# One row of exponentials per batch on ScalarE in a fused attention, gated and soft mixture kernel

## The chip, the core and the metric

One core of a Trainium2 chip runs the kernel. Its engines are TensorE (PE in the profile; PEld is its weight loads), VectorE (DVE), ScalarE (ACT), GpSimd (POOL) and SyncE (SP), which issues the DMAs here. The metric is the device time of one execution in microseconds; lower is better. Spans and rows of a profile come from one execution that the hardware profiler recorded.

## The reference

Three stages follow one another. Shapes: x is 8 batches, 8 heads, 512 tokens, 64 wide; state has 32 rows per batch and head.

```
scores  = x @ state^T / 8                 # per batch and head, 512 x 32
a       = softmax(scores, over the 32)    ; xread = a @ state
a2      = softmax(scores^T, over the 512) ; sread = a2 @ x
X       = [xread ; sread], 4352 tokens of 512
xn      = X / rms(X) * g
Y       = (silu(xn @ w_gate) * (xn @ w_val)) @ w_out     # 512 -> 1536 -> 512
logits  = Y @ phi                          # 32 slots, 4 for each of 8 experts
d       = softmax(logits, over all tokens) ; slots = d^T @ Y
out_e   = relu(slots_e @ w1_e) @ w2_e
result  = softmax(logits, over the 32 slots) @ out
```

Both softmaxes over many rows subtract a maximum first; the one over all tokens is kept as a running maximum and sum, batch by batch.

## The kernel before, in words

The work goes by batch g (a group of 512 tokens, four tiles of 128). The kernel never forms Y's input rows in full: it multiplies the attention weights A of a batch with a product of state and weights. For each batch and each of three column parts c of w_gate and w_val, `sw(b, c, gv)` makes that product in two PSUM banks; ScalarE copies each bank into the high part of a tile wp, and VectorE subtracts to get the low part, after which the banks are empty. `main_mm` (six matmuls) then makes one 128 x 512 tile of gate or val; `main_silu` (sg, on ScalarE) and `main_h` (h, on VectorE) empty it. `h_T` ("turn") transposes h by TensorE, and ScalarE or VectorE copies the result into hT. `lg_mm` gives the logits of a batch, `post1`, `post2`, `post_exp`, `post3` the running softmax (lgs is a copy of the logits, L their slots, nm the negated maximum, E the exponentials, al the factor for what came before), and `slot_h` adds to the slot sums acc on VectorE. `c_exp` and `c_norm` make the softmax over the slots.

Attention of a later batch is woven in: `att_a3` makes the scores in two banks and takes their maximum cm and a copy sT; `att_a4` makes a transposed copy a and subtracts block maxima; `att_exp` exponentiates sT and a; `att_norm` normalizes; `att_b1` turns sT into e2T; `att_b2`, `att_b3` give the state read; `att_gram`, `att_q`, `att_v`, `att_ss`, `rinv` give the rms. `wconv` converts one piece of w_out, on ScalarE, VectorE and GpSimd.

For batches 2 to 7 `steady(g)` lays a stage out by hand. A stage has 12 units (c, t); a unit is one gate and one val `main_mm`. After every second unit comes a burst, `bursts[0]` to `bursts[5]`, and `plan` puts further steps at a unit. Within these stages TensorE takes its instructions in the order of the program text (`manual_schedule`). On the other engines a scheduler fixes the order at compile time: an instruction that is ready earlier may go first, and among ready ones the one traced first. `tc.keep_in_program_order(ins)` ("pin") holds an instruction behind the one traced just before it on its engine; it doesn't hold later ones back. There are four `misc` banks (sw, turns, and all small products) and three `mm` banks (main_mm) in PSUM, and 19 buffers of 8 KB per partition, k8, for wp, h, hT and the loads. The exponential and silu use different tables of ScalarE, and a load of a table stands in the trace as ACT_TABLE_LOAD under the line of the activation that wants it.

Of the kernel before, what the change touches and what calls it, by code (L numbers as in the profile page):

```python
# [12 lines left out]
AF = mybir.ActivationFunctionType  # L13
ALU = mybir.AluOpType
AX = mybir.AxisListType
# [5 lines left out]
def kernel(  # L21
# [16 lines left out]
    nc = tc.nc  # L38
    B, P, H, NT, D = x_n.shape
# [6 lines left out]
    NC = DFF // 512  # L46
    NF = DFF // P
    ROWS = S + NS
    scale = 1.0 / float(D) ** 0.5
# [16 lines left out]
    def k4(name, shape, dt=F32):  # L66
        return att.tile([P] + shape, dt, tag="k4", bufs=5, name=name)

    def asmall(name, shape, bufs=1, dt=F32):
        return att.tile(shape, dt, tag=name, bufs=bufs, name=name)  # L70
# [4 lines left out]
    def small(name, shape, bufs=1, dt=F32):  # L75
        return sm.tile(shape, dt, tag=name, bufs=bufs, name=name)
# [4 lines left out]
    def misc():  # L81
        return psp.tile([P, 512], F32, tag="misc", bufs=4, name="misc")

    def mm(o, lhsT, rhs, start=True, stop=True):
        nc.tensor.matmul(out=o, lhsT=lhsT, rhs=rhs, start=start, stop=stop)  # L85
# [24 lines left out]
    def transpose(o, i):  # L110
        nc.tensor.transpose(o, i, ident)  # L111


    XN, T = {}, {}
# [126 lines left out]
    def att_a3(b):  # L241
        sT = k4("sT", [2, 512])
        cm = asmall("cm", [P, 2], bufs=2)
        ncm = asmall("ncm", [P, 2], bufs=2)
        pss = [misc(), misc()]
        for r in range(2):
            for hp in range(4):
                mm(
                    pss[r][32 * hp : 32 * hp + 32, :],
                    T[b, "stT"][64 * r : 64 * r + 64, 32 * hp : 32 * hp + 32],  # L250
                    T[b, "xT"][64 * r : 64 * r + 64, hp, :],
                )
            if b == 0:
                nc.scalar.copy(sT[:, r, :], pss[r])
            nc.vector.reduce_max(cm[:, r : r + 1], pss[r], axis=AX.X)
            if b > 0:
                nc.scalar.copy(sT[:, r, :], pss[r])
        nc.vector.tensor_scalar(
            out=ncm, in0=cm, scalar1=-scale, scalar2=None, op0=ALU.mult
        )  # L260
        T[b, "sT"], T[b, "ncm"] = sT, ncm

    def att_a4(b):
        sT = T[b, "sT"]
        if b > 0:
            a = k4("a", [2, 16, 32])
            rm = asmall("rm", [P, 32], bufs=2)
            nc.vector.transpose(
                a.rearrange("p r t n -> p (r t n)"), sT.rearrange("p r s -> p (r s)")
            )  # L270
            a3 = a.rearrange("p r t n -> p (r t) n")
            nc.vector.reduce_max(rm, a3, axis=AX.X)
            nc.gpsimd.tensor_tensor(
                out=a3, in0=a3, in1=rm.unsqueeze(2).to_broadcast([P, 32, 32]), op=ALU.subtract
            )
            T[b, "a"] = a
            return
        a = k4("a", [NT, 2, 4, 32])
        rm = asmall("rm", [P, NT, 2, 4], bufs=2)
        for j in range(2):  # L280
            ps = misc()
            for t2 in range(2):
                t = 2 * j + t2
                for r in range(2):
                    o = (2 * t2 + r) * P
                    transpose(ps[:, o : o + P], sT[:, r, t * P : (t + 1) * P])
            v = ps.rearrange("p (t r k n) -> p t r k n", t=2, r=2, k=4)
            rmj = rm[:, 2 * j : 2 * j + 2]
            nc.vector.reduce_max(rmj, v, axis=AX.X)
            nc.vector.tensor_tensor(  # L290
                out=a[:, 2 * j : 2 * j + 2].rearrange("p t r k n -> p (t r k) n"),
                in0=ps.rearrange("p (a n) -> p a n", n=32),
                in1=rmj.rearrange("p t r k -> p (t r k)").unsqueeze(2).to_broadcast([P, 16, 32]),
                op=ALU.subtract,
            )
        T[b, "a"] = a.rearrange("p t r k n -> p t r (k n)")
# [314 lines left out]
    def gsize(g):  # L611
        return 2 if g == sread_group else NT
# [29 lines left out]
        )  # L642
        Q[g, "L"], Q[g, "nm"], Q[g, "dm"] = L, nm, dm

    def post_exp(g):
        np_ = gsize(g) * 32
        L, nm, dm = Q[g, "L"], Q[g, "nm"], Q[g, "dm"]
        E = small("E", [P, P])
        es = small("es", [P, 1], bufs=2)
        nc.scalar.activation(  # L650
            out=E[:np_], in_=L[:np_], func=AF.Exp, bias=nm[:np_], accum_out=es[:np_]
        )
        if g > 0:
            al = small("al", [P, 1], bufs=2)
            nc.scalar.activation(out=al[:np_], in_=dm[:np_], func=AF.Exp)
            nc.vector.scalar_tensor_tensor(  # L656
                out=sacc[:np_], in0=sacc[:np_], scalar=al[:np_], in1=es[:np_],
                op0=ALU.mult, op1=ALU.add,
            )
            Q[g, "al"] = al  # L660
        else:
            nc.vector.tensor_copy(sacc, es)
        Q[g, "E"] = E
# [242 lines left out]
    def steady(g):  # L906

        nb, nn = g + 1, g + 2
        last = g == B - 1

        def turn(c, t, dve=False):
            return (h_T, g, c, t, dve)

        bursts = [[] for _ in range(6)]
        b = bursts[0]
        if g > 2:
            b += [(lg_mm, g - 1, 2, 3), (post1, g - 1)]
        b += [turn(0, 0, True), (sw, g, 1, 0), (post2, g - 1)]
        if not last:
            b += [(att_gram, nb)]  # L920
        b += [(post_exp, g - 1), (c_exp, g - 2, True)]
        b = bursts[1]
        b += [(sw, g, 1, 1)]
        if 2 < g < B - 1:
            b += [(att_b2, g)]
        b += [turn(0, 1), (post3, g - 1), turn(0, 2)]
        if not last:
            b += [(att_b1, nb)]
        b = bursts[2]
        b += [turn(0, 3), turn(1, 0)] + [(slot_h, g - 1, i) for i in range(NC)]  # L930
        if 2 < g < B - 1:
            b += [(att_b3, g)]
        if g == B - 2:
            b += [(att_b2, nb)]
        b += [(lg_mm, g, 0, 3), (sw, g, 2, 0)]
        b = bursts[3]
        b += [(sw, g, 2, 1)]
        if not last:
            b += [(att_q, nb, 0), (att_q, nb, 1)]
        b += [turn(1, 1), turn(1, 2)]  # L940
        if g == B - 2:
            b += [(att_b3, nb)]
        b = bursts[4]
        if nn < B:
            b += [(att_a3, nn)]
        b += [turn(1, 3)]
        if not last:
            b += [(att_v, nb), (att_ss, nb), (rinv, nb), (sw, nb, 0, 0)]
        else:
            b += [turn(2, 0)]  # L950
        if g == B - 2:
            b += [(sread_sum,)]
        b = bursts[5]
        if not last:
            b += [(sw, nb, 0, 1), turn(2, 0), (lg_mm, g, 1, 3), turn(2, 1), turn(2, 2), turn(2, 3, True)]
            if g == B - 2:
                b += [(sread_prep2,)]
            ended.add(g)
        else:
            b += [turn(2, 1), (lg_mm, g, 1, 3), turn(2, 2)]  # L960

        at = lambda u, slot, f, *a: plan.setdefault((base + u, slot), []).append((f, a))
        at(2, 1, c_norm, g - 2)
        if not last:
            at(1 if g == B - 2 else 7, 1, load_xn, nb)
            at(1, 1, att_exp, nb, True)
            at(2, 1, att_norm, nb)
            at(4, 1, att_b4, nb)
            at(6, 1, att_g, nb)
            at(1, 1, wload, 1)  # L970
            at(4, 1, wconv, 1)
        if nn < B:
            at(8, 1, load_xt, nn)
            at(9, 1, att_z, nn)
            at(11, 1, att_a4, nn)
        if g == B - 2:
            at(8, 1, sread_prep)
        if last:
            at(0, 2, prefetch, 2)
            at(8, 1, prefetch, 2)  # L980
            at(11, 1, w_split, 0, 0)
            at(12, 2, w_split, 1, 0)

        return bursts

    for s, units in enumerate(stages):
        def at(u, slot, f, *a):
            plan.setdefault((base + u, slot), []).append((f, a))
# [65 lines left out]
        elif s == 1:  # L1054
            g = s
# [9 lines left out]
            nb = g + 1  # L1065
# [14 lines left out]
            nb = g + 2  # L1080
# [4 lines left out]
        else:  # L1085
            if s == 2:
                pe_order.enter_context(tc.manual_schedule(engines={mybir.EngineType.PE}))
            bursts = steady(s)
# [56 lines left out]
    for u, (c, gv) in enumerate(halves):  # L1145
# [56 lines left out]
        out=dsel, in0=mg, scalar1=mrun, scalar2=0.0, op0=ALU.subtract, op1=ALU.max  # L1202
# [45 lines left out]
    for e in range(NE):  # L1248
        es = slice(4 * e, 4 * e + 4)
        nc.vector.tensor_tensor(  # L1250
            out=sinE[e][:, :, es],
            in0=ps[:, :P].rearrange("p (k s) -> p k s", k=4)[:, :, es],
# [164 lines left out]
    def out0_end(t, ps, copy):  # L1417
# [15 lines left out]
        out=so[64:], in0=ps[64:], in1=so_h[64:].bitcast(F32), op=ALU.subtract  # L1433
# [58 lines left out]
```

## Time and profile before

| what | us |
|---|---|
| median of three runs | 664.88 (663.0 to 666.22) |
| the profiled execution, its own time | 665.96 |
| its span in the profile | 664.1 |

The granted clock of TensorE is 0.97 of full speed over the span. The stages of batches 2 to 7 lie between about 190 and 545 us of the span; the stage of batch 4 begins near 309.5, that of batch 7 near 486.5. A row of the timeline gives start, duration (of all that is merged in it), engine, line, operation, what is written from what, the count, and in brackets how long the engine had been idle and what ended that.

### The profile page before, as it was taken

The page shows a single profiled execution, that of the slowest core. Times are in us where ns is not written, and L with a number is a line of the kernel's source. Part 1 is how long each engine was busy: PE and PEld are TensorE (multiplying, and loading weights), DVE is VectorE, ACT ScalarE, POOL GpSimd, SP SyncE. Part 2 cuts the span into 40 slices and gives each one's busy share as a digit, 9 for nine tenths or more (in the row PEclk, how much of TensorE's full clock was granted, in tenths as well). Part 3 has the DMA queues.
Part 4 walks back from the last instruction along what each step waited for, and adds up shares of the span by engine and source line. Part 5 has one row for each costly group of instructions (what it writes and reads, how often), then busy time and mean ns, then how long its engine had stood idle before and what let it go on. Part 6 is the DMA issues. An engine that isn't in the chain of part 4 may idle for free.

```text
span 664.1 us, 11195 instructions
## 1 busy us (share of the span) xinstructions
PE 613.4 (92%) x4432; PEld 386.4 (58%) x4432; DVE 437.3 (66%) x874; ACT 349.5 (53%) x558; POOL 157.3 (24%) x178
## 2 busy tenths in 40 slices
PE   6679988899998999999999999999999999999990
PEld 4336555456566556666656656666765777653350
DVE  6979999576587776766868585685765365252161
ACT  5467773475268447534843763484346476311170
POOL 2645455342032311401141040113000000003420
PEclk9697999799999999999999999999999999999996
DMA  8950065131020410031040104300270327999757
GB/s 354 416 207 1 1 254 191 63 127 68 1 81 16 163 51 14 21 143 64 1 164 12 53 1 159 128 1 34 102 279 3 126 84 274 318 332 402 301 207 331
DMA packets 32715, 92.14 MB, mean 139 GB/s; under 512 B 1816, under 2 KB 3224, under 8 KB 29848
## 3 DMA queue, kind: packets, MB, share of 16 engines
q1 hardware_dynamic: 32376, 91.36, 37.2%
q8 instruction: 35, 0.57, 0.4%
q14 instruction: 16, 0.13, 0.1%
q10 hardware_dynamic: 288, 0.07, 0.0%
HBM read 79.37 MB, written 12.06 MB: 138 GB/s over the span
## 4 chain that ended last, share of the span: by engine, by line
PE 68%; DVE 11%; ACT 7%; issue 2%; POOL 0%; DVEq 0%; ACTq 0%
PE mm L85 38%; PE misc L85 15%; PE misc L111 9%; PE lg L85 4%; PE so L85 2%; DVE wp L538 2%; DVE h L574 1%; DVE w L204 1%; ACT L566 1%; ACT sg L566 1%; ACT wp L537 1%; ACT L650 1%; DVE wo L204 1%; DVE sacc L656 1%; DVE w L212 1%
## 5 line engine op out<-in xcount | busy, mean ns | idle before, releaser
L85 PE MATMUL mm<-wp,A 128*128 128x512 f32 x1152 | 286.3, 401 | 3.8 <-DVE h L574 2.4
L85 PEld LDWEIGHTS mm<-wp,A 128*128 128x128 f32 x1152 | 213.3, 190 | 75.4 <-issue 23.4
L574 DVE SCALAR_TENSOR_TENSOR h<-mm,rinv,sg 128x512 f32<-128x512 f32 x102 | 76.0, 747 | 87.3 <-PE mm L85 81.8
L566 ACT ACTIVATE sg<-mm,rinv 128x512 f32<-128x512 f32 x102 | 70.5, 692 | 103.0 <-PE mm L85 90.7
L537 ACT CAST wp<-misc 128x512 fp32r<-128x512 f32 x96 | 51.5, 590 | 65.3 <-PE misc L85 65.3
L538 DVE TENSOR_TENSOR wp<-misc,wp 128x512 fp32r<-128x512 f32 x96 | 62.2, 684 | 24.8 <-ACT wp L537 24.7
L85 PE MATMUL misc<-w,stTg 64*32 64x512 f32 x768 | 67.1, 626 | 12.0 <-POOL w L216 6.6
L585 ACT COPY hT<-misc 128x512 f32<-128x512 f32 x87 | 48.9, 591 | 41.3 <-PE misc L111 35.5
L111 PEld LDWEIGHTS misc<-ident,h 128*128 128x128 f32 x408 | 45.7, 142 | 32.3 <-DVE h L574 10.6
L111 PE MATMUL misc<-ident,h 128*128 128x128 f32 x408 | 59.1, 282 | 4.0 <-ACT hT L585 2.1
L216 POOL TENSOR_TENSOR w<-w,raw 128x512 int32<-128x512 int32 x20 | 28.3, 1426 | 29.2 <-DVE w L212 7.1
L85 PEld LDWEIGHTS misc<-w,stTg 64*32 64x32 f32 x768 | 10.9, 106 | 37.1 <-issue 15.4
L85 PE MATMUL mm<-wh,xsg 128*128 128x512 f32 x96 | 31.8, 400 | 0.0
L511 POOL TENSOR_TENSOR rinv<-ri,rs_magic 128x4 int32<-128x4 int32 (+1 forms) x9 | 1.8, 197 | 122.1 <-DVE ri L507 122.0
L216 POOL TENSOR_TENSOR wo<-wo,raw 128x512 int32<-128x512 int32 x18 | 24.7, 1385 | 22.7 <-DVE wo L212 7.0
L468 POOL TENSOR_TENSOR A<-aT,A 128x1024 fp32r<-128x1024 f32 x7 | 16.9, 2411 | 46.1 <-ACT A L467 46.1
L85 PE MATMUL lg<-hT,wphi 128*32 128x512 f32 (+1 forms) x216 | 27.5, 579 | 0.0
L85 PE MATMUL misc<-h,ET 128*32 128x512 f32 x204 | 26.4, 596 | 0.0
L1238 POOL MEMSET sinE<- 128x512 f32 x2 | 1.0, 524 | 106.2 <-PE mm L85 96.1
L566 ACT ACT_TABLE_LOAD x18 | 23.1, 1283 | 0.3
L191 ACT ACTIVATE raw<-raw 128x1024 int32<-128x1024 uint32 x19 | 22.1, 1161 | 0.0
L85 PEld LDWEIGHTS mm<-wh,xsg 128*128 128x128 f32 x96 | 17.9, 188 | 6.7 <-issue 3.1
(221 smaller groups left out, 845.2 us busy)
## 6 DMA issues: line engine op xcount, KB each, us to landing
ew<-in_w_dram SPq DMA_DIRECT2D x27, 1024.0 KB, 6.7
xT<-in_x_t_dram SPq DMA_DIRECT2D x8, 1024.0 KB, 7.6
xn<-in_x_n_dram SPq DMA_DIRECT2D x8, 1024.0 KB, 6.4
raw<-in_w_val_dram SPq DMA_DIRECT2D x6, 1024.0 KB, 15.9
raw<-in_w_out_dram SPq DMA_DIRECT2D x6, 1024.0 KB, 5.1
out_dram<-ob SPq DMA_DIRECT2D x6, 1024.0 KB, 10.4
ew_w<-in_w_dram SPq DMA_DIRECT2D x5, 1024.0 KB, 9.3
raw<-in_w_gate_dram SPq DMA_DIRECT2D x4, 1024.0 KB, 13.8
```

The costliest lines, as they stand in the source:

```text
L85: nc.tensor.matmul(out=o, lhsT=lhsT, rhs=rhs, start=start, stop=stop)
L111: nc.tensor.transpose(o, i, ident)
L191: ins = nc.scalar.activation(out=rnd, in_=lo.bitcast(U32), func=AF.Copy, scale=2.0 ** -29)
L204: nc.vector.tensor_scalar(out=dst[:, h], in0=dst[:, h], scalar1=EXP_LO, scalar2=EXP_HI, op0=ALU.max, op1=ALU.min,)
L212: nc.vector.scalar_tensor_tensor(out=a[:, h], in0=hi[:, h], scalar=-0x40000000, in1=a[:, h], op0=ALU.bitwise_and, op1=ALU.bitwise_or,)
L216: nc.gpsimd.tensor_tensor(out=a[:, h], in0=a[:, h], in1=rnd[:, h], op=ALU.add)
L468: nc.gpsimd.tensor_tensor(out=A[:, :, 1, :], in0=aT, in1=A[:, :, 0, :].bitcast(F32), op=ALU.subtract)
L537: nc.scalar.copy(t[:, r, 0, :], ps)
L538: nc.vector.tensor_tensor(out=t[:, r, 1, :], in0=ps, in1=t[:, r, 0, :].bitcast(F32), op=ALU.subtract)
L566: nc.scalar.activation(out=sg, in_=ps, func=AF.Silu, scale=RINV[g][:, t : t + 1])
L574: nc.vector.scalar_tensor_tensor(out=HH[g, c][:, t, :], in0=ps, scalar=RINV[g][:, t : t + 1], in1=sg, op0=ALU.mult, op1=ALU.mult,)
L585: (nc.vector.tensor_copy if on_dve else nc.scalar.copy)(HT[g, c][:, :, t * P : (t + 1) * P], ps.rearrange("p (q n) -> p q n", q=4))
```

## The change

In `steady`, `sw(g, 1, 0)` becomes the first step of the first burst and `sw(g, 1, 1)` moves from the second burst into the first. `post_exp` is pinned; attention's exponentials for the next batch (`att_exp`) move from the plan of unit 1 to a place right behind it, ahead of `c_exp`. The second burst keeps `att_b2`, one turn, whose copy goes from ScalarE to VectorE, and `post3`, and gets `sw(g, 2, 0)` from the third. The third burst interleaves turns and slot products and takes `att_b1`. In batch 6's stage the state read of the last batch, its preparation and its sums move one burst later. For batches 4 to 7 (`b > 3`) `att_a3` only copies the scores; the maximum, over both halves in one instruction, is taken from the copy in `att_a4`. For batches 1 to 3 the maximum is taken as before.

```diff
--- before.py
+++ after.py
@@ -252,13 +252,15 @@
                 )
             if b == 0:
                 nc.scalar.copy(sT[:, r, :], pss[r])
-            nc.vector.reduce_max(cm[:, r : r + 1], pss[r], axis=AX.X)
+            if b <= 3:
+                nc.vector.reduce_max(cm[:, r : r + 1], pss[r], axis=AX.X)
             if b > 0:
                 nc.scalar.copy(sT[:, r, :], pss[r])
-        nc.vector.tensor_scalar(
-            out=ncm, in0=cm, scalar1=-scale, scalar2=None, op0=ALU.mult
-        )
-        T[b, "sT"], T[b, "ncm"] = sT, ncm
+        if b <= 3:
+            nc.vector.tensor_scalar(
+                out=ncm, in0=cm, scalar1=-scale, scalar2=None, op0=ALU.mult
+            )
+        T[b, "sT"], T[b, "ncm"], T[b, "cm"] = sT, ncm, cm
 
     def att_a4(b):
         sT = T[b, "sT"]
@@ -274,6 +276,12 @@
                 out=a3, in0=a3, in1=rm.unsqueeze(2).to_broadcast([P, 32, 32]), op=ALU.subtract
             )
             T[b, "a"] = a
+            if b > 3:
+                cm = T[b, "cm"]
+                nc.vector.reduce_max(cm, sT, axis=AX.X)
+                nc.vector.tensor_scalar(
+                    out=T[b, "ncm"], in0=cm, scalar1=-scale, scalar2=None, op0=ALU.mult
+                )
             return
         a = k4("a", [NT, 2, 4, 32])
         rm = asmall("rm", [P, NT, 2, 4], bufs=2)
@@ -642,17 +650,21 @@
         )
         Q[g, "L"], Q[g, "nm"], Q[g, "dm"] = L, nm, dm
 
-    def post_exp(g):
+    def post_exp(g, pin=False):
         np_ = gsize(g) * 32
         L, nm, dm = Q[g, "L"], Q[g, "nm"], Q[g, "dm"]
         E = small("E", [P, P])
         es = small("es", [P, 1], bufs=2)
-        nc.scalar.activation(
+        ins = nc.scalar.activation(
             out=E[:np_], in_=L[:np_], func=AF.Exp, bias=nm[:np_], accum_out=es[:np_]
         )
+        if pin:
+            tc.keep_in_program_order(ins)
         if g > 0:
             al = small("al", [P, 1], bufs=2)
-            nc.scalar.activation(out=al[:np_], in_=dm[:np_], func=AF.Exp)
+            ins = nc.scalar.activation(out=al[:np_], in_=dm[:np_], func=AF.Exp)
+            if pin:
+                tc.keep_in_program_order(ins)
             nc.vector.scalar_tensor_tensor(
                 out=sacc[:np_], in0=sacc[:np_], scalar=al[:np_], in1=es[:np_],
                 op0=ALU.mult, op1=ALU.add,
@@ -913,34 +925,37 @@
 
         bursts = [[] for _ in range(6)]
         b = bursts[0]
+        b += [(sw, g, 1, 0)]
         if g > 2:
             b += [(lg_mm, g - 1, 2, 3), (post1, g - 1)]
-        b += [turn(0, 0, True), (sw, g, 1, 0), (post2, g - 1)]
+        b += [turn(0, 0, True), (sw, g, 1, 1), (post2, g - 1)]
         if not last:
             b += [(att_gram, nb)]
-        b += [(post_exp, g - 1), (c_exp, g - 2, True)]
+        b += [(post_exp, g - 1, True)]
+        if not last:
+            b += [(att_exp, nb, True)]
+        b += [(c_exp, g - 2, True)]
         b = bursts[1]
-        b += [(sw, g, 1, 1)]
         if 2 < g < B - 1:
             b += [(att_b2, g)]
-        b += [turn(0, 1), (post3, g - 1), turn(0, 2)]
+        b += [turn(0, 1, True), (post3, g - 1), (sw, g, 2, 0)]
+        b = bursts[2]
+        b += [turn(0, 2), (slot_h, g - 1, 0), turn(0, 3), (slot_h, g - 1, 1)]
+        b += [turn(1, 0), (slot_h, g - 1, 2), (lg_mm, g, 0, 3)]
         if not last:
             b += [(att_b1, nb)]
-        b = bursts[2]
-        b += [turn(0, 3), turn(1, 0)] + [(slot_h, g - 1, i) for i in range(NC)]
         if 2 < g < B - 1:
             b += [(att_b3, g)]
-        if g == B - 2:
-            b += [(att_b2, nb)]
-        b += [(lg_mm, g, 0, 3), (sw, g, 2, 0)]
         b = bursts[3]
         b += [(sw, g, 2, 1)]
         if not last:
             b += [(att_q, nb, 0), (att_q, nb, 1)]
         b += [turn(1, 1), turn(1, 2)]
         if g == B - 2:
+            b += [(att_b2, nb)]
+        b = bursts[4]
+        if g == B - 2:
             b += [(att_b3, nb)]
-        b = bursts[4]
         if nn < B:
             b += [(att_a3, nn)]
         b += [turn(1, 3)]
@@ -949,11 +964,12 @@
         else:
             b += [turn(2, 0)]
         if g == B - 2:
-            b += [(sread_sum,)]
+            b += [(sread_prep,)]
         b = bursts[5]
         if not last:
             b += [(sw, nb, 0, 1), turn(2, 0), (lg_mm, g, 1, 3), turn(2, 1), turn(2, 2), turn(2, 3, True)]
             if g == B - 2:
+                b.insert(1, (sread_sum,))
                 b += [(sread_prep2,)]
             ended.add(g)
         else:
@@ -963,7 +979,6 @@
         at(2, 1, c_norm, g - 2)
         if not last:
             at(1 if g == B - 2 else 7, 1, load_xn, nb)
-            at(1, 1, att_exp, nb, True)
             at(2, 1, att_norm, nb)
             at(4, 1, att_b4, nb)
             at(6, 1, att_g, nb)
@@ -973,8 +988,6 @@
             at(8, 1, load_xt, nn)
             at(9, 1, att_z, nn)
             at(11, 1, att_a4, nn)
-        if g == B - 2:
-            at(8, 1, sread_prep)
         if last:
             at(0, 2, prefetch, 2)
             at(8, 1, prefetch, 2)
```

## Rows read from the trace of the kernel before

**Rows 1.** The page's busy time, share and instructions by engine.

```profile
PE 613.4 (92%) x4432; PEld 386.4 (58%) x4432; DVE 437.3 (66%) x874; ACT 349.5 (53%) x558; POOL 157.3 (24%) x178
```

**Rows 2.** TensorE's waits, 190 to 545 us: waiter, releaser, total us, times, longest.

```profile
PE misc L85 <- ACT sT L257: 2.9, 4, 0.7
PE misc L111 <- ACT hT L585: 2.1, 1, 2.1
PE misc L669 <- DVE wp L538: 1.8, 4, 0.4
PE misc L111 <- DVE wp L538: 1.2, 5, 0.6
```

**Rows 3.** Timeline of batch 4's stage, TensorE: start, duration, instruction, idle before.

```profile
314.93 1.07 PE L85 MATMUL lg<-hT,wphi 128*32 128x512 f32 x8
...
316.51 1.09 PE L85 MATMUL misc<-w,stTg 64*32 64x512 f32 x16
...
317.53 0.42 PE L85 MATMUL misc<-lgs,r 128*32 128x128 f32 x8
...
318.00 5.74 PE L85 MATMUL mm<-wp,A 128*128 128x512 f32 x24
...
326.82 0.33 PE L669 MATMUL misc<-ident,E 128*128 128x128 f32 x1 [0.44 <-DVE wp L538]
...
328.70 5.74 PE L85 MATMUL mm<-wp,A 128*128 128x512 f32 x24
...
334.29 1.03 PE L111 MATMUL misc<-ident,h 128*128 128x128 f32 x8
...
335.25 2.78 PE L85 MATMUL misc<-h,ET 128*32 128x512 f32 x24
...
357.66 1.09 PE L85 MATMUL misc<-w,stTg 64*32 64x512 f32 x16 [0.73 <-ACT sT L257]
```

**Rows 4.** The same timeline, ScalarE.

```profile
315.74 0.72 ACT L302 ACTIVATE sT<-sT,ncm 128x512 f32<-128x512 f32 x1
...
318.11 1.05 ACT L537 CAST wp<-misc 128x512 fp32r<-128x512 f32 x2
...
320.48 0.69 ACT L566 ACTIVATE sg<-mm,rinv 128x512 f32<-128x512 f32 x1
...
321.19 1.28 ACT L650 ACT_TABLE_LOAD   x1
...
322.48 0.40 ACT L650 ACTIVATE E<-L,nm 128x128 f32<-128x128 f32 x1
...
323.29 1.28 ACT L566 ACT_TABLE_LOAD   x1
...
356.93 0.59 ACT L257 COPY sT<-misc 128x512 f32<-128x512 f32 x1 [2.42 <-DVE cm L255]
```

**Rows 5.** The same timeline, VectorE.

```profile
316.07 0.69 DVE L617 COPY lgs<-lg 128x512 f32<-128x512 f32 x1 [0.20 <-PE lg L85]
...
326.09 1.28 DVE L538 TENSOR_TENSOR wp<-misc,wp 128x512 fp32r<-128x512 f32 x2
...
333.08 2.04 DVE L204 TENSOR_SCALAR wo<-wo 128x512 f32<-128x512 f32 x2 [0.50 <-ACT wo L188]
...
337.58 2.05 DVE L693 SCALAR_TENSOR_TENSOR acc<-acc,al,misc 128x512 f32<-128x512 f32 x3
...
356.21 1.29 DVE L255 TENSOR_REDUCE cm<-misc 128x1 f32<-128x512 f32 x2 [0.20 <-PE misc L85]
```

**Rows 6.** Timeline of batch 7's stage, from 494 us.

```profile
496.08 0.28 DVE L630 COPY L<-misc 128x128 f32<-128x128 f32 x1
...
496.79 0.69 ACT L566 ACTIVATE sg<-mm,rinv 128x512 f32<-128x512 f32 x1 [0.86 <-PE mm L85]
...
497.33 0.15 DVE L640 TENSOR_SCALAR nm<-cmx 128x1 f32<-128x1 f32 x1
```

**Rows 7.** Waits of the SP queue that issues loads, 480 to 664 us.

```profile
SPq L821 <- PE mm L85: 42.6, 14, 5.8
```

## The prediction

> **What bounds the kernel now.** I read the page's busy shares first: TensorE is busy 613.4 of 664.1 us, VectorE 66%, ScalarE 53%, GpSimd 24% [rows 1]. So an edit to ScalarE's or VectorE's order pays only where TensorE stands still for it. The second view was therefore TensorE's own waits over the six stages that `steady` lays out (batches 2 to 7): the four that count are 2.9 + 2.1 + 1.8 + 1.2 = 8.0 us in 355 us [rows 2]. That is the whole prize; nothing else in these stages can come off TensorE, because the change removes no matmul. Third, the timeline of one stage (batch 4) showed where the waits lie; its PE rows [rows 3], ACT rows [rows 4] and DVE rows [rows 5] are to be read side by side. In PE's, the first burst runs from 314.93 to 318.00 without a gap; in the second, `post3` stood 0.44 us on VectorE's `wp`; in the fifth, `sw` stood 0.73 us on ScalarE's `sT` copy.
>
> Why `wp` is late: ScalarE runs attention's three exponentials (315.74 to 318.11), then two `wp` copies (to 319.16), a table load, sg (320.48), a table load (321.19), the softmax exponentials (322.48), a table load (323.29) and the next sg. Only after that does it empty the second pair of `sw` banks. Four `misc` banks turn round, so the fourth allocation after each of those two finds its bank still being emptied.
>
> **The change, part by part.** I lay it out on a clock of its own: t = 0 is TensorE's start of the first burst (314.93 in rows 3).
>
> TensorE's pieces: sw 1.02 (316.51 to 317.53); lg_mm with turn(0,0) 1.58 (314.93 to 316.51); post2 with att_gram 0.47 (317.53 to 318.00); four main_mm some 5.7 (5.74 with the last one's end), 1.42 each; a turn 0.5 (eight transposes in 1.03, four to a turn); a slot product 0.9 (2.78 for three) [rows 3].
>
> *First burst, one sw longer.* TensorE: sw(1,0) 0 to 1.0, lg_mm and turn to 2.6, sw(1,1) to 3.6, post2 and gram. VectorE has to empty in that time: two `wp` remainders (1.28 a pair), lgs (0.69), hT (priced as lgs: the same 512 columns out of a bank) [rows 5]. The first copy on ScalarE lands at about 1.7, so VectorE finishes at 1.7 + 1.28 + 0.6 + 0.7 = 4.3. post2 needs lgs (3.6, just in time), and gram needs the bank that hT leaves at 4.3, where TensorE would have been at 3.9: a new stop of 0.4 us in each of five stages (batch 7 has no gram): **+2.0**. The lower bound is 0, if another bank is handed out; the upper 0.7, one more VectorE copy ahead: 0 to +3.5.
>
> *The row of exponentials.* Pins only hold an instruction behind what is traced before it on its engine; sg of the third unit is traced later and free to go first, as it did past the pinned c_exp, which ran between 322.48 and 323.29, after the sg of 320.48 [rows 4]. Which is ready first? sg: gram at 4.3, then 0.2 and one main_mm of 1.42: 6.0. post_exp: batch 7's stage, which has no attention part, gives the chain from L to nm as 496.08 to 497.48, 1.4 us with one `wp` remainder inside; sg stood ready there at 496.79 and went first [rows 6]. Here both remainders and gram's product lie within it, about 0.8 us more, and L starts at 4.3: 6.4 or 6.5. So sg goes first by some 0.4 us, and the row follows: sg to 6.7, a load 1.3, softmax exponentials and c_exp 0.81 (322.48 to 323.29), attention's three 2.37 (315.74 to 318.11), a load 1.3, second sg done at 13.1 [rows 4]. TensorE runs units three and four from 4.5 to 10.2, then the second burst to 13.1 (before it took 5.0, from 318.00 + 5.7 to 328.70; the two waits, 0.6, a turn and att_b1's eight transposes, 1.5, leave it: 2.9); its fifth unit's val, at 14.5, is the first that needs the bank of that sg. 1.4 us to spare: **0**. Four table loads a stage become two; ScalarE's 2.6 us are not on TensorE's path. If that cover is gone, the price is the first rival's.
>
> *What leaves the stretch.* sw(1,1) no longer waits for the row, turn(0,1) is emptied by VectorE, and att_b1 (with ScalarE's e2T copy) goes a burst later. The waits on `wp` and on `hT` go: **−(1.8 + 1.2 + 2.1) = −5.1** [rows 2]. Bounds: −5.1 and 0. VectorE takes over one copy a stage (0.69, as lgs); its bank is asked for four allocations on, by the third burst's first turn at t = 18.8, 6 us later, and that covers it.
>
> *Scores copied first.* Now VectorE's maximum (1.29 for the pair) reads the bank before ScalarE may copy it; the copy started 356.93 though the scores were there at 356.21 [rows 3, 4, 5]. After, the two copies start 0.7 us earlier and the next sw finds its banks empty, while the maximum runs over `sT` after the block maxima. It applies to att_a3 of batches 4 to 7: **−2.9** [rows 2]. Both maxima become one instruction over 1024 columns; priced at twice the single one it costs VectorE nothing net, and what needs it, attention's exponential, comes only in the next stage's row, which covers its delay. Bounds −2.9 and 0.
>
> *sw(2,0), the slot products, att_b1, att_b2 of batch 7, the state read's sums moved.* TensorE does the same pieces. The interleaved turns and slot products bring a tighter bank order: acc is emptied behind the weight conversion, which holds VectorE from 333.08 to the start of acc at 337.58 [rows 5]. I charge 0.1 us in five stages, **+0.5**; bounds 0 and 1.5 us a stage (second rival). Queues: load_xn, load_xt, wload keep their places, and no DMA is added.
>
> Sum: 2.0 − 5.1 − 2.9 + 0.5 = −5.5 us. The profiled execution took 665.96 (span 664.1 and 1.9 around it), so 660.5; the median shown is 664.88, 1.1 lower, which gives 659.4. I take 660. The tail passes this on: the expert loads wait for TensorE to free buffers, not TensorE for them [rows 7].
>
> The Trainium skill ("ScalarE: Activation LUTs", section "What ACT_TABLE_LOAD costs") gives a switch of sets 1.28 us for the load and 1.38 for a drain. The trace has 1.29 from a load's start to the next activation, 321.19 to 322.48, and the sg ahead of the load ended at 321.17 [rows 4]: no drain of that size. By the page, the second sg would come 2.7 us later, at 15.8, and stop TensorE 1.3 us a stage, which would make some 667 of the forecast; as the loads in the same rows say otherwise, I give that no chance.
>
> **The rivals.**
> 1. *Slower: post_exp goes ahead of sg.* If nm is ready first in the order that the scheduler fixes, the whole row stands before the third unit's sg: 6.4 + 0.81 + 2.37 + 1.3 + 0.7 = 11.6. There are three `mm` banks, so unit four's val, due at 4.5 + 3 × 1.42 = 8.8, waits 2.8 us. In five stages +14: −5.5 + 14 = +8.5, 673 to 674. For it: the margin is only 0.4 us, and the fix is made before the chip runs. Against: both stages shown have sg first, and there too it was traced later [rows 4, 6]. It decides from the point where the chain from L to nm gets under 1.7 us. Chance 0.20.
> 2. *A bank in the third burst.* If slot product 2 gets the bank of slot product 0 (strict turn: it needs acc's first, which in before ended at 338.3, t = 23.4), and TensorE asks at 13.1 + 5.7 + 3.4 = 22.2, it stops 1.2 us, 1.5 with later conversions, in five stages: +6 to +7.5. Sum about +1: 665 to 667, or 663 if it hits less. For it: that VectorE queue. Against: the hT bank in between is empty by then, and no such stop stands in rows 2, though acc was as late. Chance 0.20.
> 3. *The forecast*, its bounds 656.9 (all 8.0 gone, nothing new) and 662.5 (gram at 0.7, the third burst at half a microsecond). Chance 0.60.
>
> **How the numbers follow.** A measurement of this kernel can tell about 0.5%, 3.3 us. Nearly all of the forecast's case lies below 661.6: faster 0.58. The second rival is within 0.5%, with the forecast's upper edge: same 0.22. Rival 1: slower 0.20. The range 656 to 669 holds the forecast and rival 2, and rival 1 only where it strikes in few of the five stages; the forecast's own is 656 to 663.
>
> **What would show it.** Right: TensorE's waits on `wp` in post3, on `hT` and on `sT` gone; two table loads in a stage, sg / row / sg on ScalarE; a wait of 0.4 us in gram on hT; a stage 0.9 us shorter. Wrong: a wait of a main_mm on sg of 2 to 3 us (rival 1), or a slot product waiting on acc (rival 2). The same PE gaps in other places would make me wrong by the bank order; an unchanged 0.73 at sw would mean that the copies do not start at the end of the scores.

## The result, and the profile after

The changed kernel took 673.39 us (median of four runs, 671.52 to 673.62) against 664.38 (four runs, 663.0 to 666.22): ratio 1.0128, 95% interval 1.0096 to 1.0159. It is slower by 9 us, where 660 was forecast and 656 to 669 was the range. The profiled execution took 673.62, with a span of 671.5 and a granted clock of 0.97, as before. Over the six stages the granted clock is 1.00 in both traces (190 to 545 us before, 189.5 to 552 after), so a slower clock is not the reason.

The page's busy line of the changed kernel answers to [rows 1]:

```profile
PE 623.6 (93%) x4432; PEld 387.0 (58%) x4432; DVE 433.7 (65%) x876; ACT 334.4 (50%) x542; POOL 159.6 (24%) x178
```

TensorE runs the same 4432 instructions and is busy 10.2 us longer. ScalarE lost sixteen instructions and 15 us; it was never the bound. TensorE's waits over the same stages, now at 190 to 552 us (waiter, releaser, total us, times, longest), answer to [rows 2]:

```profile
PE misc L111 <- ACT hT L593: 2.8, 5, 0.7
PE misc L85 <- DVE hT L593: 1.1, 4, 0.3
PE mm L85 <- ACT sg L574: 0.5, 1, 0.5
PE misc L85 <- ACT sT L258: 0.3, 1, 0.3
```

These are 4.7 us, where [rows 2] has 8.0. By this view the kernel should be faster. So the loss had to be looked for inside TensorE's busy time, by the lengths of the bursts. A burst is counted here from the start of its first instruction to the start of the next `main_mm`. From the start of unit 0 of batch 2 to the end of the last main_mm of batch 7 it was 344.4 us (190.30 to 534.69) and is 352.5 (189.52 to 542.05), 8.1 more. The stages start 0.8 earlier, the tail is as long as before, and the span grew by 7.4. The table shows where the 8.1 lie, over the six stages. The third column is what a burst gains or loses because a step moved into it or out of it, with each step at its length in before (sw 1.02, a turn 0.49, att_b1 0.79, and of the state read of batch 7 and its sums 1.03, 0.11 and 0.57); the last column is the real change.

| stretch | change of its length | of it moved steps | the rest |
|---|---|---|---|
| first bursts | +10.2 | +6.1 | +4.1 |
| second bursts | −9.7 | −6.9 | −2.8 |
| third bursts | +7.0 | −0.3 | +7.2 |
| fourth bursts | +0.9 | +0.9 | 0 |
| fifth bursts | −1.0 | −0.5 | −0.5 |
| sixth bursts | +0.6 | +0.6 | 0 |
| main_mm | +0.1 | 0 | +0.1 |

The timeline of batch 4's stage, TensorE, answers to [rows 3]:

```profile
317.96 1.09 PE L85 MATMUL misc<-w,stTg 64*32 64x512 f32 x16
...
319.73 0.32 PE L85 MATMUL misc<-bdt,stT 128*32 128x64 f32 x8 [0.26 <-DVE hT L593]
...
327.49 1.99 PE L85 MATMUL misc<-w,stTg 64*32 64x512 f32 x16
329.40 5.78 PE L85 MATMUL mm<-wp,A 128*128 128x512 f32 x24
...
337.13 1.06 PE L85 MATMUL misc<-h,ET 128*32 128x512 f32 x8
338.82 0.66 PE L111 MATMUL misc<-ident,h 128*128 128x128 f32 x4 [0.62 <-ACT hT L593]
...
341.26 1.31 PE L111 MATMUL misc<-ident,sT 128*128 128x128 f32 x8
...
342.66 5.74 PE L85 MATMUL mm<-wp,A 128*128 128x512 f32 x24
...
359.42 1.46 PE L85 MATMUL misc<-w,stTg 64*32 64x512 f32 x16
```

The same form, a `sw` of sixteen records, lasts 1.09 at 317.96, 1.99 at 327.49 and 1.46 at 359.42, and no bracket stands at it. Narrow windows show why. First comes the sw of the third burst of before, then the one at 327.49, in two windows 1 us apart:

```profile
339.22 0.66 PE L85 MATMUL misc<-w,stTg 64*32 64x512 f32 x8
```

```profile
327.49 0.63 PE L85 MATMUL misc<-w,stTg 64*32 64x512 f32 x4
...
328.41 0.63 PE L85 MATMUL misc<-w,stTg 64*32 64x512 f32 x4
```

`sw` fills two banks from the two halves of the rows (64 rows each). In before, both halves start in the same half microsecond; after, one half starts alone and the other 0.92 us later. By the trace TensorE works all the time, but with half of its rows: the waits of its matmuls don't show this. The rows of its weight loads (PEld) do, and they name what the second half waited for, srd on VectorE. First the load in batch 4, then the line of the weight loads' waits over the stages, 189.5 to 552 us:

```profile
328.41 0.15 PEld L85 LDWEIGHTS misc<-w,stTg 64*32 64x32 f32 x8 [0.77 <-DVE srd L368]
```

```profile
PEld misc L85 <- DVE srd L368: 3.1, 4, 0.8
```

The Trainium skill ("TensorEngine Tiling (Array Packing)", section "Key Properties") says that tiles work independently and in parallel. The trace agrees as far as both banks are free: 1.02 us for both halves, 1.92 where the second bank came late.

Why srd was late is read on VectorE, whose rows answer to [rows 5]:

```profile
321.78 0.14 DVE L648 TENSOR_SCALAR nm<-cmx 128x1 f32<-128x1 f32 x1
...
326.66 1.22 DVE L334 TENSOR_REDUCE asum<-a 128x32 f32<-128x1024 f32 x1 [0.58 <-ACT a L323]
...
328.07 0.28 DVE L368 TENSOR_TENSOR srd<-misc,rs 128x128 f32<-128x128 f32 x1
...
328.64 0.66 DVE L593 COPY hT<-misc 128x512 f32<-128x512 f32 x1
...
336.70 1.98 DVE L204 TENSOR_SCALAR wo<-wo 128x512 f32<-128x512 f32 x2 [1.57 <-ACT wo L188]
...
341.13 2.05 DVE L705 SCALAR_TENSOR_TENSOR acc<-acc,al,misc 128x512 f32<-128x512 f32 x3
```

and on ScalarE, to [rows 4]:

```profile
321.68 0.69 ACT L574 ACTIVATE sg<-mm,rinv 128x512 f32<-128x512 f32 x1 [1.51 <-PE mm L85]
322.39 1.28 ACT L658 ACT_TABLE_LOAD   x1
...
325.59 1.04 ACT L323 ACTIVATE a<-a 128x1024 f32<-128x1024 f32 x1
...
328.14 0.69 ACT L574 ACTIVATE sg<-mm,rinv 128x512 f32<-128x512 f32 x1
...
334.53 1.05 ACT L475 CAST A<-aT 128x1024 fp32r<-128x1024 f32 x1 [2.73 <-DVE aT L472]
335.49 1.18 ACT L188 ACTIVATE wo<-raw 128x1024 f32<-128x1024 f32 x1
336.57 1.17 ACT L191 ACTIVATE raw<-raw 128x1024 int32<-128x1024 uint32 x1
337.62 0.68 ACT L574 ACTIVATE sg<-mm,rinv 128x512 f32<-128x512 f32 x1
338.19 1.07 ACT L593 COPY hT<-misc 128x512 f32<-128x512 f32 x2
```

The row stands as forecast: sg, one table load, all exponentials, one load, sg; sg at 321.68 began 0.24 us before nm was done (321.92). But attention's exponential `a` now ends at 326.63. Two chains hang on it. VectorE's sums over it (`att_norm`, asum) stand in VectorE's order ahead of srd and of the hT copy of turn(0,1): VectorE is idle 0.58 until `a` is there, takes 1.22, and srd, which empties the bank of att_b2, ends at 328.35: sw's second half starts 0.06 later, at 328.41. And normalizing, transposing and casting A come later, and behind them ScalarE's part of `wconv`, which runs from 335.49 to 337.74, amid the third burst's turns; the hT copies follow from 338.19, and turn(1,0) stands 0.62 us. VectorE's part of the conversion then starts at 336.70, where it was 333.08, and acc at 341.13, where it was 337.58 [rows 5]. The second half of att_b1 waits for acc, again in the weight loads alone:

```profile
341.92 0.42 PEld L111 LDWEIGHTS misc<-ident,sT 128*128 128x128 f32 x4 [0.24 <-DVE acc L705]
```

### The profile page after: what moved, and what is told of

The parts are those of the page before. It is cut to its first block, busy times and chain, and to the rows that moved or that the text cites. A ratio compares the mean times of both kernels' runs of the same rounds, so it can differ in the third digit from the quotient of the medians.

```text
span 671.5 us, 11183 instructions
## 1 busy us (share of the span) xinstructions
PE 623.6 (93%) x4432; PEld 387.0 (58%) x4432; DVE 433.7 (65%) x876; ACT 334.4 (50%) x542; POOL 159.6 (24%) x178
## 4 chain that ended last, share of the span: by engine, by line
PE 68%; DVE 18%; ACT 8%; issue 3%; DMA 2%; POOL 1%; DVEq 0%; ACTq 0%; POOLq 0%
PE mm L85 38%; PE misc L85 15%; PE misc L111 9%; PE lg L85 3%; DVE wp L546 3%; PE so L85 2%; DVE w L212 2%; DVE w L204 2%; DVE w L208 1%; ACT sg L574 1%; DVE aT L472 1%; ACT wo L188 1%; DVE h L582 1%; DVE asum L334 1%; DVE wo L212 1%
## 5 line engine op out<-in xcount | busy, mean ns | idle before, releaser
L85 PE MATMUL misc<-w,stTg 64*32 64x512 f32 x768 | 72.4, 620 | 9.4 <-POOL w L216 6.3
L593 ACT COPY hT<-misc 128x512 f32<-128x512 f32 x81 | 45.4, 591 | 35.7 <-PE misc L111 23.1
L85 PE MATMUL misc<-h,ET 128*32 128x512 f32 x204 | 28.9, 602 | 0.0
L337 POOL TENSOR_TENSOR a<-a,asum 128x1024 f32<-128x1024 f32 x7 | 13.4, 1916 | 35.7 <-ACT sg L574 23.0
```

The lines of the kernel that those rows point to most:

```text
L593: (nc.vector.tensor_copy if on_dve else nc.scalar.copy)(HT[g, c][:, :, t * P : (t + 1) * P], ps.rearrange("p (q n) -> p q n", q=4))
```

## The experiments

Three theories and their rivals were tried, with the letters that expectations may use. S: the scores' early copy is worth little, since the fifth burst's sw still runs with halves in series. C: the third burst's loss is the weight conversion that the later row pushes into it. D: the second burst's loss is VectorE's order, asum ahead of the copies that free banks. The rival of each is that the loss belongs to the tighter bank order itself and would move on. A last pair asked whether the row, as such, costs anything (R). Each ratio is to the kernel before as it ran beside that version (medians 665.0 to 665.82).

**Scores copied first, alone, on the kernel before.** The edit is the `att_a3` and `att_a4` part of the change, nothing of `steady`.

> The kernel before, with only the scores copied first (batches 4 to 7: maximum taken later from the copy). Theory S (a state product sw needs both of its banks at its start: if the second is late, its two halves of eight matmuls run one after the other, 1.92 us instead of 1.02): the fifth burst goes from 3.61 to about 3.3 us, not to 2.9, in four stages, so -1.2 us in all, about 663. Rival (the forecast's term): the wait of 0.73 us goes entirely, burst 2.9 us, -2.9 us, about 661.5.

663.72 us; ratio 0.9972 (0.9954 to 0.9989). The fifth burst went from 3.61 to 3.25 in four stages and nothing else moved by more than 0.05: −1.4 us in place of the −2.9 forecast. TensorE's rows in batch 4's stage:

```profile
356.14 1.46 PE L85 MATMUL misc<-w,stTg 64*32 64x512 f32 x16
357.53 4.83 PE L85 MATMUL mm<-wp,A 128*128 128x512 f32 x20
```

The 0.73 us of idle time before sw [rows 3] are gone from the matmuls' waits, but sw now takes 1.39 us instead of 1.02: half of the saved wait is spent in it. Its second half waits for the second copy:

```profile
356.53 0.15 PEld L85 LDWEIGHTS misc<-w,stTg 64*32 64x32 f32 x8 [0.24 <-ACT sT L258]
```

The early copy pays, by half of its price.

**The conversion two units later, on the changed kernel.**

```diff
-            at(4, 1, wconv, 1)
+            at(6, 1, wconv, 1)
```

> The changed kernel, with the conversion of w_out planned at unit 6 instead of unit 4. Theory C (in the third burst the hT copies on ScalarE and the acc updates on VectorE stand behind the conversion, which the later row of exponentials pushed into that burst): the third burst falls from 7.65 to about 6.4 us (only the turn and slot alternation stays, +0.4 against the old order), -1.2 us in five stages, -6 us, about 667.5, less what the conversion costs where it then runs. Rival B (the third burst's loss is its order of banks alone): the burst stays at 7.65 and the time at 673.

666.78 us; ratio 1.0024 (1.0 to 1.0047). Third bursts went from 7.65 to 6.51 in four stages, 5.0 us over all; no other burst but the fifth of batch 3 (3.58 to 3.30) changed by 0.1. This one line takes back 6.9 of the 8.5 us by which the change is slower by its ratio (1.28% of 664.4; 0.24% is left); by the traces the stages became 5.2 shorter, and the medians' interval of some 2 us holds both. TensorE's turn(1,0), and the main_mm behind the burst:

```profile
336.22 0.66 PE L111 MATMUL misc<-ident,h 128*128 128x128 f32 x4
...
339.62 1.64 PE L85 MATMUL mm<-wp,A 128*128 128x512 f32 x6
```

No bracket stands at the turn now: the 0.70 us there are gone, and the 0.39 by which att_b1 was longer (1.32 against 0.93). Those two are 1.09 of the 1.14 by which this burst is shorter in batch 4.

**sw(2,0) back at the end of the third burst, on the changed kernel.**

```diff
-        b += [turn(0, 1, True), (post3, g - 1), (sw, g, 2, 0)]
+        b += [turn(0, 1, True), (post3, g - 1)]
...
+        b += [(sw, g, 2, 0)]
         b = bursts[3]
```

> The changed kernel, with sw(2,0) back at the end of the third burst. Theory S: in the second burst sw(2,0) lost 0.90 us in five stages because the bank of its second half came late; moved, the second burst falls from 3.75 to about 1.8 to 1.9 us (its own 1.02 and the 0.90), the third grows by 1.0 (or more where acc empties its banks late, 1.9): between -4.5 us and 0. Rival (the lateness follows from the row, whatever stands there): another step of the second burst takes the wait over and the sum of both bursts stays at 11.4 us.

673.1 us; ratio 1.0114 (1.0083 to 1.0146), no different from the change. The second burst fell to 1.66, without any loss, and the third rose to 9.64: together 11.30 against 11.39, and main_mm between them took 0.2 us longer. By the trace the stages are 1.9 us longer than those of the change. The third burst, TensorE:

```profile
335.95 0.66 PE L111 MATMUL misc<-ident,h 128*128 128x128 f32 x4 [0.54 <-ACT hT L593]
...
340.28 1.66 PE L85 MATMUL misc<-w,stTg 64*32 64x512 f32 x16 [0.33 <-DVE acc L705]
```

The lost time moved on with sw: now acc holds its bank. As long as the conversion stands there, the place of sw is no cure.

**sw(1,1) behind post3 in the second burst, on the kernel before.** It leaves ScalarE's row where it is and gives its copies time.

```diff
-        b += [(sw, g, 1, 1)]
         if 2 < g < B - 1:
             b += [(att_b2, g)]
-        b += [turn(0, 1), (post3, g - 1), turn(0, 2)]
+        b += [turn(0, 1), (post3, g - 1), (sw, g, 1, 1), turn(0, 2)]
```

> The kernel before, with one step moved: sw(1,1) behind post3 in the second burst instead of at its head; exponentials as before. If the waits of the second burst (0.84 us in batches 3 to 6, 2.1 in batch 2, 0.6 in batch 7) come from banks asked for again while ScalarE is late with the wp copies, asking for them after post3 takes away most of them: burst 5.03 to about 4.4 us, -4 to -5 us in all, about 660. Rival: the wait moves on to att_b1's second bank (wp copied behind sg) and the burst stays within 0.2 us of 5.03; time 664.

663.47 us; ratio 0.9973 (0.9954 to 0.9991). The second burst went from 5.03 to 4.74 in four stages: neither the whole of the waits, nor nothing. The waits became a sw with halves partly in series, 1.25 us to the next step:

```profile
323.83 1.32 PE L85 MATMUL misc<-w,stTg 64*32 64x512 f32 x16
```

In batches 2 and 7 the main_mm behind the second burst became 1.6 and 0.8 us longer. In batch 7 it stood twice for the later wp, 0.33 us on ScalarE's copy and 0.35 on VectorE's remainder. In batch 2 it ran without a gap, but the granted clock was 0.80 between 209 and 216 us, where before had 1.00; just ahead of it a turn had stood 1.80 us. So the stages as a whole are as long as before (344.6 us against 344.4), and the gain of the medians is not one of the stages. Inconclusive as to the waits' worth; it shows the same form of loss in the order of before.

**att_norm planned two units later, on the version with the later conversion** (`at(4, 1, att_norm, nb)` for `at(2, 1, ...)`), to take asum out of the second burst.

> The changed kernel with the conversion at unit 6 (as in the run before, 666.8), and besides attention's normalization planned at unit 4 instead of unit 2. Theory D (in the second burst VectorE, which takes its instructions in a fixed order, stands at asum until the row's last exponential is done, and srd and the copy of turn(0,1), which free the banks for sw(2,0), stand behind it; sw then runs its halves one after the other): the second burst falls from 3.75 to 2.85 us in batches 3 to 6, -3.6 us, about 663. Rival (the lateness comes from srd or the turn themselves): burst unchanged, 666.8.

668.22 us; ratio 1.0029 (1.0002 to 1.0055). A miss as an experiment: the scheduler still put asum (323.20) ahead of srd (324.53) on VectorE, and the second burst stayed at 3.65.

**asum pinned behind the copy of turn(0,1), on the version with the later conversion.** A new last argument of `att_norm` pins it.

```diff
-        b += [turn(0, 1, True), (post3, g - 1), (sw, g, 2, 0)]
+        b += [turn(0, 1, True)]
+        if not last:
+            b += [(att_norm, nb, None, True)]
+        b += [(post3, g - 1), (sw, g, 2, 0)]
...
-            at(2, 1, att_norm, nb)
```

> The changed kernel with the conversion at unit 6, and attention's asum held on VectorE behind the copy of turn(0,1) (in the run before, the new place in the plan did not move asum behind it). Theory D (srd and the copy of turn(0,1) free the banks of sw(2,0), and stand behind asum, which waits for the row's last exponential): the second burst falls from 3.75 to about 2.85 us in batches 3 to 6, -3.6 us against the run with the conversion at unit 6 (666.8), about 663. Rival: 3.65 to 3.75 stays, and the time.

663.74 us; ratio 0.9981 (0.9959 to 1.0004). The second burst fell from 3.75 to 2.94 in four stages, and sw to 1.10. VectorE, then TensorE's sw:

```profile
321.90 0.28 DVE L370 TENSOR_TENSOR srd<-misc,rs 128x128 f32<-128x128 f32 x1
...
322.51 0.68 DVE L595 COPY hT<-misc 128x512 f32<-128x512 f32 x1
323.11 1.21 DVE L334 TENSOR_REDUCE asum<-a 128x32 f32<-128x1024 f32 x1
```

```profile
322.13 1.17 PE L85 MATMUL misc<-w,stTg 64*32 64x512 f32 x16
```

asum now runs behind srd and the copy, and the halves run together, although the row of exponentials stands as in the changed kernel. Given the later row, VectorE's order is the cause.

**The third burst in blocks** (three turns, three slot products, att_b1, att_b3, lg_mm, sw(2,0)), on the version with the later conversion.

```diff
-        b += [turn(0, 1, True), (post3, g - 1), (sw, g, 2, 0)]
+        b += [turn(0, 1, True), (post3, g - 1)]
...
-        b += [turn(0, 2), (slot_h, g - 1, 0), turn(0, 3), (slot_h, g - 1, 1)]
-        b += [turn(1, 0), (slot_h, g - 1, 2), (lg_mm, g, 0, 3)]
+        b += [turn(0, 2), turn(0, 3), turn(1, 0)] + [(slot_h, g - 1, i) for i in range(NC)]
...
+        b += [(lg_mm, g, 0, 3), (sw, g, 2, 0)]
```

> The changed kernel with the conversion at unit 6, sw(2,0) back at the end of the third burst, and that burst in blocks again: three turns, three slot products, att_b1, att_b3, lg_mm, sw(2,0). Theory S with C (with the conversion out of the way acc empties its banks in time, and blocks save the 0.3 us of alternation): second plus third burst fall from 3.75 + 6.51 = 10.26 to about 1.7 + 7.2 = 8.9 us in five stages, -6.5 to -7 us, about 660. Rival (sw(2,0) finds its second bank late at the new place as well, 1.92 us): 9.8, -2 us, about 664.5.

662.87 us; ratio 0.9955 (0.993 to 0.998). Second 1.66 and third 7.3, together 8.96, against 10.26 in the version it starts from: 0.9 is the sw that ran in series, and some 0.4 the alternation; 0.25 is given back in the main_mm ahead of the third burst (5.60 to 5.85). TensorE's rows of the block:

```profile
331.16 1.47 PE L111 MATMUL misc<-ident,h 128*128 128x128 f32 x12
332.56 2.78 PE L85 MATMUL misc<-h,ET 128*32 128x512 f32 x24
335.28 1.10 PE L111 MATMUL misc<-ident,sT 128*128 128x128 f32 x8
```

Three turns and three slot products take 4.12 us in blocks (331.16 to 335.28) and took 4.57 by turns, 333.12 to 337.69, in the version with the later conversion.

**att_gram in the second burst behind post3, on the version in blocks.** It takes gram from behind the copy of turn(0,0).

> As the run in blocks, and besides att_gram goes from the first burst to the second, behind post3. If the first burst's 0.5 us over its work is gram waiting for the bank that VectorE empties last (turn(0,0)), the first burst falls from 4.63 to 3.9, of which 0.25 is gram itself and comes back in the second: -0.45 us in five stages, some 2.3 us below the run in blocks, about 657.5. Rival (what is late is sw(1,1)'s or post2's own bank): the first burst falls by gram's 0.25 alone and the time stays.

661.5 us; ratio 0.9934 (0.9912 to 0.9956). The first burst fell from 4.63 to 4.04, the second rose by 0.42, which is gram itself, and the third by 0.15: nothing, net. What shows in the medians (−1.4, less than expected) is main_mm ahead of the third burst, back from 5.85 to 5.58.

**A turn ahead of the next batch's sw in the fifth burst, on that version** (turn(1,3) copied by VectorE, turn(2,0) ahead of sw(next,0,0)).

> As the run in blocks with att_gram in the second burst (661.5), and in the fifth burst turn(1,3) is copied by VectorE and turn(2,0) comes ahead of sw(next,0,0), so that both banks of that sw are empty when it starts. Theory S: its step falls from 1.39 to 1.02 us, the fifth and sixth burst together from 7.19 to about 6.8 us in the four stages with scores, -1.5 us, about 660. Rival (the copies of the scores come late for any bank): 7.2 stays.

661.3 us; ratio 0.993 (0.9904 to 0.9956). TensorE:

```profile
350.94 0.66 PE L111 MATMUL misc<-ident,h 128*128 128x128 f32 x4
351.52 1.11 PE L85 MATMUL misc<-w,stTg 64*32 64x512 f32 x16
```

sw has its halves together again, and fifth and sixth burst went from 7.19 to 6.75 in four stages. The stages are 1.6 us shorter by the trace; the medians of the two, 661.5 and 661.3, can't tell that. The copy on VectorE and the new place of the turn were not tried one by one. It is the fastest version that was run, by its median and by its stages, ahead of the kernel before (665.82 beside it) and of the change.

**The row split again: attention's exponentials back in the plan of unit 1, on the version with gram moved.**

> As the run in blocks with att_gram in the second burst (661.5), with attention's exponentials back at unit 1, ahead of the wp copies, as in the kernel before: four table loads a stage instead of two, and the row split. Theory R (the row pays here by letting the wp copies go first, not by the saved loads): sw(1,1) finds the bank of its second half 1.5 to 2 us late, the first burst grows from 4.04 to 5.5 or 6 us in five stages, about 670. Rival (ScalarE has slack enough for both orders): first burst within 0.3 us of 4.04, 661 to 663.

666.58 us; ratio 1.002 (0.9997 to 1.0043). The first burst rose from 4.04 to 5.32:

```profile
317.73 1.06 PE L85 MATMUL misc<-w,stTg 64*32 64x512 f32 x8
319.09 1.06 PE L85 MATMUL misc<-w,stTg 64*32 64x512 f32 x8 [0.30 <-DVE hT L593]
```

sw(1,1) runs wholly in series. In the repaired order the one row is worth about 5 us by the medians and 6.2 by the stages: the expectation's direction, at some 0.6 of its size by the medians. The split brings back both the two table loads and the exponentials ahead of the wp copies; no run parts the two.

All versions side by side, the length of the six stages by the trace and the median:

| version | stages | median |
|---|---|---|
| before | 344.4 | 664.38 |
| the change | 352.5 | 673.39 |
| scores copied first alone, on before | 342.9 | 663.72 |
| sw(1,1) later, on before | 344.6 | 663.47 |
| sw(2,0) back | 354.4 | 673.1 |
| conversion later | 347.4 | 666.78 |
| and att_norm planned later | 347.3 | 668.22 |
| conversion later, asum pinned | 344.1 | 663.74 |
| conversion later, third burst in blocks | 342.3 | 662.87 |
| and gram moved | 341.1 | 661.5 |
| and a turn ahead of sw | 339.5 | 661.3 |
| gram moved, the row split again | 347.3 | 666.58 |

Unit 0 of batch 2 starts between 186.5 and 190.3 us in these twelve traces, so single executions differ by up to 3.8 us ahead of the stages; a small gain is better read from the stages.

## Why the prediction was wrong

The step that failed is the price of 0.1 us a stage for the third burst. It left out attention, which reads the row's last exponentials, and the conversion behind it: that burst lost 7.2 us in all. Under it lies the opening premise that only waits can change, since no matmul is removed: TensorE's busy time rose by 10.2 us with the same 4432 instructions.

Its terms, with what the stages of the changed kernel measured (from the last column of the table above; of the fifth bursts' −0.5, +0.43 is batch 6's sw, which ran in series, and the rest belongs to the scores):

| term | forecast | measured |
|---|---|---|
| First burst, one sw longer | +2.0 | +4.1 |
| The row of exponentials | 0 | one wait of 0.5 (batch 7), counted with main_mm |
| What leaves the stretch | −5.1 | −2.8 |
| Scores copied first | −2.9 | −1.0 |
| sw(2,0), the slot products, att_b1 moved | +0.5 | +7.2 |
| sw in batch 6's fifth burst; main_mm | 0 | +0.6 |
| sum | −5.5 | +8.1 |

*sw(2,0), the slot products, att_b1 … moved: the step "I charge 0.1 us in five stages" failed by most.* It treated the third burst as a question of banks alone and took acc's time from the trace of before. But attention's part of the row, over at 318.1 before [rows 4], ends at 326.63, 8.5 us later, and the conversion, planned behind the cast of A, moved with it, by 3.6 us, into the burst. The prediction followed the row only to the second sg ("1.4 us to spare") and not to its other reader, attention. Moving the conversion took 5.0 us out of these bursts.

*What leaves the stretch.* The second bursts' waits on `wp` and `hT` did go. What failed is that nothing would be late in their place: sw(2,0), called the same piece of work, took 1.92 us instead of 1.02, 0.90 in each of four stages, and that ate the 0.84 saved there. The working priced VectorE's added copy by the bank that it holds, and didn't ask which banks sw(2,0) would get: one is that of srd, behind asum. Batches 2 and 7, which saved 2.2 and 0.7, are all of the gain. Pinning asum behind the copy gave back 3.3 us.

*Scores copied first.* Mechanism right, size wrong: −1.4 alone, half of the wait, because a bank freed late in sw's run still splits its halves; −1.0 within the change, where one stage of four gained nothing (fifth burst of batch 3, 3.61 to 3.58).

*First burst.* The stop in gram on hT is there, 0.26 of idle time and 0.53 us of burst (forecast 0.4) in batches 3 to 6. Batches 2 and 7 lost 1.0 each: there sw(1,1) ran in series, in batch 2 behind VectorE's wp remainder:

```profile
199.78 0.15 PEld L85 LDWEIGHTS misc<-w,stTg 64*32 64x32 f32 x8 [0.73 <-DVE wp L546]
```

*The row of exponentials* was priced right as far as sg goes: sg went first, by 0.24 us where 0.4 was forecast, and no main_mm waited for the second sg in batches 2 to 6. What the row costs through attention stands under the third burst.

*The rivals.* The measured time is the one that the first rival gives, 673 to 674, and that is chance: its mechanism didn't occur. The second rival had the right place and size (1.2 to 1.5 us a third burst) but another step, slot product 2 on acc; what stood was turn(1,0) on ScalarE's hT copies, and att_b1. It came to only 666 because it kept the gains of 8 us whole. The forecast's upper edge, 662.5, was summed 0.4 too low: gram at 0.7 and the third burst at half a microsecond add 1.5 and 2.0 to the −5.5, which from 664.88 gives 662.9.

With the conversion and asum put right, the stages stand at −0.3 us by the same table (first bursts +4.1, second −6.1, third +2.3, scores −1.2, the rest +0.6) and the ratio at 0.9981. So the forecast's case, too, was priced some 5 us too well: by the stops and the halves in series in the first bursts, the latter in the fifth bursts too, and by the alternation in the third (2.3 where 0.5 was charged). The gain that the versions after it have comes from orders that undo parts of the change and keep the row.

Not settled: whether asum's wait and the conversion add up simply (no run has asum alone moved), and how far the 0.4 us of alternation in the third burst come from changing tile shapes rather than from the order of banks; the blocks changed both.

## What to carry to other kernels

When a producer is moved later, list every reader of its results, and everything that is queued behind those readers on their engines; what was planned at a fixed place will slide with them into a stretch that was chosen for other work. Weigh a saved wait at the step that waits next: where a step fills several banks at once, its price is set by when the last bank is free. Compare lengths of stretches between the same landmarks in both traces before believing a view of waits, and read the waits of the weight loads beside those of the matmuls.

## What was not expected of the hardware

A group of matmuls over two row halves slowed from 1.02 to 1.25, 1.39 and 1.92 us in the runs here as its second bank came later, with no idle time on TensorE in the trace: in the changed kernel busy time rose by 10.2 us with the same 4432 instructions, while the waits of the six stages fell from 8.0 to 4.7 us. TensorE's weight loads name the late bank: they stood 3.1 us, in four stages, for srd. And alternating transposes (128 x 128 tiles) with slot products (128 x 32 tiles) took 0.45 us more than the same six steps in blocks, whose order of banks was another too.
